# A recurrent attention layer with a gated MLP behind it: the sign of each weight set in an activation, narrow first projections for two more chunks, and another written order

## The chip, the cores and the metric

One core of one Trainium2 chip runs the whole kernel in a single launch. The metric is the device time of an execution in microseconds, lower is better. TensorE (PE) multiplies matrices, VectorE (DVE), ScalarE (ACT) and GpSimd (POOL) do elementwise work, SyncE (SP) issues all DMAs from one queue. Each engine works through its own instructions in the order in which the program lists them.

## The reference, cut to what matters

```
# q, k, v, o_gate: (4, 8, 768, 40); i_gate, f_gate: (4, 8, 768); all fp32
for t in range(S):
    m_new = max(f_gate[t] + m, i_gate[t])
    f, i = exp(f_gate[t] + m - m_new), exp(i_gate[t] - m_new)
    C = f * C + i * outer(v[t], k[t])          # per batch and head
    n = f * n + i * k[t]
    y[t] = sigmoid(o_gate[t]) * (C @ q[t]) / max(abs(n . q[t]), 1)
x = y as (3072 tokens, 320)
h = x @ w_in                                   # w_in (320, 2048)
g = h * erf(softplus(h))
out = g @ w_out                                # w_out (2048, 320)
```

In the reference's inputs w_in and w_out are float64 numbers; the host only reinterprets them as 64-bit integers, and the kernel turns them into fp32 itself.

## The kernel before, in words

The recurrence is worked in 12 chunks of 64 time steps (NC = 12, L = 64). A chunk's tokens are 4 batches x 64 steps = 256; they are handled in two pairs of batches (r = 0, 1), each 128 tokens. For a pair the kernel loads queries and keys (`qk`) and keys, values and output gates (`kvo`), multiplies scores with a decay mask (`dm`, L563), makes the local products, the products with the state and the state's update (L517, L522, L531), divides, gates, transposes (L390 to L394) and splits the result into a rounded half `xh` and a rest `xl`. A gate block (`gate_block`) does the scans of the gates for two chunks and writes small sums to DRAM, from where they are broadcast into `dm` and `eT`.

The MLP of a chunk has four groups g, each for 4 of the 16 blocks of 128 hidden columns. Groups 0 to 7 belong to the first two chunks, alternating; group g from 8 on belongs to chunk g // 4. A group has up projections (L751), evictions to `hb` (L762, in the wide form also L767), softplus, erf and a product with `hb` (L771, L775, L779), a split of that into `gh` and `gl` (L789 or L791, L795; groups 0 to 5 are "plain" and have none), and down projections (L815 plain, L817 to L820 split) into an accumulator per chunk that is stored after the fourth group.

An up projection adds weight half x input half products. In the narrow form a step does two blocks of 128 hidden columns with 8 matmuls of 256 tokens each, all into the block's own half of a 512-column tile, and one ScalarE copy of 512 columns evicts both. In the wide form a step does one block with 5 matmuls: three that have both input halves side by side as 512 moving columns, and two of 256. The two halves of the tile then have to be added: ScalarE copies one to `hb` and VectorE adds the other (L767). Before, groups from 8 on are wide.

A weight arrives as pairs of 32-bit words, 26 pieces in all (8 from `weights_in`, 2 from `weights_tail`, 16 from `weights_out`), by way of `raw` tiles. `decode` makes fp32 bits of it: VectorE shifts the low words (L625), ScalarE multiplies the high words, read as fp32, by 2^-112 (L631), VectorE shifts that left by 3 and joins it with the low word (L636), and VectorE takes the sign bit of the high word and joins that too (L638). `halves`, `weights_tail` and `split_out` split the result into halves.

The order of all this is written out by hand: `ORDER` is a list of step numbers, and each step's instructions are issued when its turn comes. The steps' costs in the program belong to the planner that made the list and issue nothing. A negative entry issues filler matmuls. Where a ScalarE step names table sets (X is the exponential set, S softplus, G the sigmoid set) and the loaded one isn't among them, `Plan.run` issues a load of the first named set (L878). A load waits for its buffer, a step for its inputs, and whatever is queued behind on the same engine waits with it; `raw`, `qk`, `kvo`, `hb` and some others share a pool of 20 buffers.

Of the kernel before, what the change touches and what calls it, by code (L numbers as in the profile page):

```python
# [13 lines left out]
ALU = mybir.AluOpType  # L14
# [16 lines left out]
REBIAS = 2.0 ** -112  # L31


class Plan:
# [138 lines left out]
def tile_mlstm_moe(  # L173
# [446 lines left out]
    def decode(key, raw, n, full, out, **first):  # L620
# [7 lines left out]
        @op('ACT', n / 1010 + 0.063, r=[(R, 0)], w=[(R, 2)])  # L628
        def _():
            word = raw().bitcast(F32)[:, :, 1]  # L630
            nc.scalar.activation(word, word, AF.Copy, scale=REBIAS)  # L631

# [307 lines left out]
```

## Time and profile before

| | before |
|---|---|
| time, median of 3 runs | 468.57 us (466.16 to 469.02) |
| the profiled execution | 470.77 us |
| its span, first to last instruction | 469.1 us |
| TensorE busy | 453.2 us (97%), 6010 matmuls, granted clock 0.985 |
| VectorE busy | 358.8 us (77%), 713 instructions |
| ScalarE busy | 334.2 us (71%), 541 instructions, 57 of them table loads of 73.1 us |
| DMA | 51.80 MB, 110 GB/s on average |

The busy share of TensorE is an upper bound: matmuls are pipelined, and the ends of their records are modelled. What the span is made of is told by stretches and gaps.

### The profile page before, as it was taken

To read this page: it belongs to the slowest core of one execution; us is meant where nothing else is said; L and a number is where in the kernel's file an instruction comes from. 1 tells how busy PE (TensorE), PEld (TensorE's weight loads), DVE (VectorE), ACT (ScalarE), POOL (GpSimd) and SP (SyncE) were. 2 spreads that over 40 slices of the span, in tenths; PEclk is the share of its full clock that TensorE was granted. 3 is DMA by queue.
4 is the path that set the end of the run, shared out by engine and by line. 5 is a ranking of instruction groups with operands and counts; after the bars stand their busy time and mean duration, and the time that the engine had idled before them with its cause. 6 is when DMAs were issued, how large, how long until landed. Compare 5 with 4: busy or idle time off the path is not lost.

```text
span 469.1 us, 13982 instructions
## 1 busy us (share of the span) xinstructions
PE 453.2 (97%) x6010; PEld 397.6 (85%) x6010; DVE 358.8 (77%) x713; ACT 334.2 (71%) x541; POOL 35.8 (8%) x62
## 2 busy tenths in 40 slices
PE   8798997999999999999999999999999999999996
PEld 4467995788788898898899898888899889999996
DVE  6979999789997876878749786786579659665762
ACT  5746988788997486787658985775796584566650
POOL 2001040002010230000210010015000000000000
PEclk9979999899999999999999999999999999999999
DMA  7988876095335703235305612543232100000011
GB/s 219 385 233 288 239 200 199 16 236 185 92 84 149 180 3 83 76 84 148 105 4 147 162 25 88 144 117 116 92 89 82 31 1 1 15 1 14 16 43 28
DMA packets 46830, 51.80 MB, mean 110 GB/s; under 512 B 27056, under 2 KB 31664, under 8 KB 46768
## 3 DMA queue, kind: packets, MB, share of 16 engines
q1 hardware_dynamic: 46768, 50.91, 37.6%
q8 instruction: 47, 0.77, 0.7%
q14 instruction: 15, 0.12, 0.1%
HBM read 46.77 MB, written 4.13 MB: 109 GB/s over the span
## 4 chain that ended last, share of the span: by engine, by line
PE 73%; DVE 10%; DMA 8%; ACT 4%; SPq 2%; issue 2%; DVEq 0%; ACTq 0%
PE h L751 29%; PE pob L819 10%; PE pob L817 9%; PE pob L820 9%; PE pa L815 3%; DMA dm<-gd 3%; PE pa L531 2%; PE pa L508 2%; DMA eT<-gd 2%; PE pa L517 2%; PE pob L815 2%; DMA raw<-in_w_in_dram 2%; DVE raw L636 1%; PE pa L390 1%; PE pa L522 1%
## 5 line engine op out<-in xcount | busy, mean ns | idle before, releaser
L751 PE MATMUL h<-xh,wh 128*128 128x512 f32 (+1 forms) x672 | 203.7, 371 | 2.0 <-DVE hb L767 1.2
L751 PEld LDWEIGHTS h<-xh,wh 128*128 128x128 f32 x672 | 114.9, 189 | 20.8 <-DVE hb L767 2.6
L762 ACT ACTIVATE hb<-h 128x256 f32<-128x256 f32 (+1 forms) x176 | 69.2, 399 | 74.5 <-PE h L751 74.1
L767 DVE TENSOR_TENSOR hb<-h,hb 128x256 f32<-128x256 f32 x160 | 66.3, 420 | 60.6 <-ACT hb L762 59.6
L751 PE MATMUL h<-xh,wl 128*128 128x256 f32 x384 | 108.0, 281 | 0.0
L819 PE MATMUL pob<-woh,gh 128*128 128x320 f32 x328 | 98.3, 311 | 0.0
L820 PE MATMUL pob<-wo,gh 128*128 128x320 f32 x328 | 97.5, 309 | 0.0
L751 PEld LDWEIGHTS h<-xh,wl 128*128 128x128 f32 x384 | 72.7, 189 | 2.8
L878 ACT ACT_TABLE_LOAD x57 | 73.1, 1283 | 1.8 <-PEq L928 0.8
L779 DVE TENSOR_TENSOR n<-n,hb 128x1024 f32<-128x1024 f32 x48 | 58.9, 1230 | 6.7 <-ACT n L775 6.4
L820 PEld LDWEIGHTS pob<-wo,gh 128*128 128x128 f32 x328 | 61.6, 188 | 1.7
L819 PEld LDWEIGHTS pob<-woh,gh 128*128 128x128 f32 x328 | 61.6, 188 | 0.4
L817 PE MATMUL pob<-woh,gl 128*128 128x320 f32 x328 | 60.7, 311 | 0.0
L486 POOL TENSOR_SCALAR_AFFINE_SELECT dm<-dm 128x512 f32<-128x512 f32 (+1 forms) x40 | 32.3, 815 | 290.4 <-ACT dm L466 266.0
L817 PEld LDWEIGHTS pob<-woh,gl 128*128 128x128 f32 x328 | 52.4, 188 | 1.9
L771 ACT ACTIVATE n<-hb 128x1024 f32<-128x1024 f32 x48 | 49.9, 1056 | 3.9 <-DVE hb L767 2.1
L795 DVE TENSOR_TENSOR gl<-n,gh 128x1024 fp32r<-128x1024 f32 x42 | 52.1, 1246 | 0.3
L775 ACT ACTIVATE n<-n 128x1024 f32<-128x1024 f32 x48 | 50.2, 1055 | 0.3
L789 ACT ACTIVATE gh<-n 128x1024 fp32r<-128x1024 f32 x26 | 27.4, 1055 | 2.7 <-DVE n L779 2.7
L407 DVE TENSOR_TENSOR xh<-pa,xh 128x384 fp32r<-128x384 f32 x24 | 13.3, 553 | 13.2 <-ACT xh L403 13.2
L825 ACT ACTIVATE o<-pob 128x320 f32<-128x320 f32 x22 | 9.4, 433 | 16.2 <-PE pob L817 13.9
L403 ACT ACTIVATE xh<-pa 128x384 fp32r<-128x384 f32 x24 | 11.7, 488 | 11.9 <-PE pa L394 7.0
(98 smaller groups left out, 510.9 us busy)
## 6 DMA issues: line engine op xcount, KB each, us to landing
qk<-in_qk_dram SPq DMA_DIRECT2D x24, 512.0 KB, 4.9
kvo<-in_kvo_dram SPq DMA_DIRECT2D x24, 484.0 KB, 4.0
eT<-gd SPq DMA_DIRECT2D x44, 128.0 KB, 4.0
raw<-in_w_out_dram SPq DMA_DIRECT2D x16, 320.0 KB, 4.7
dm<-gd SPq DMA_DIRECT2D x40, 128.0 KB, 3.8
raw<-in_w_in_dram SPq DMA_DIRECT2D x8, 512.0 KB, 7.0
out_dram<-o SPq DMA_DIRECT2D x48, 80.0 KB, 2.4
raw<-in_w_in_dram SPq DMA_DIRECT2D x4, 256.0 KB
```

The costliest lines, as they stand in the source:

```text
L486: nc.gpsimd.affine_select(out=x, in_=x, pattern=[[0, H], [1, L]], compare_op=ALU.is_ge, fill=0.0, base=base, channel_multiplier=-1)
L751: nc.tensor.matmul(h[:, n * T:n * T + n_], w, m, start=(s == 0), stop=(s == len(ops) - 1))
L762: nc.scalar.activation(part(), G(f'h{i}')[:, T:2 * T] if wide else G(f'h{i}'), AF.Copy)
L767: nc.vector.tensor_tensor(part(), G(f'h{i}')[:, 0:T], part(), op=ALU.add)
L771: nc.scalar.activation(new('n0', [128, 1024], ('n0', g)), G('hb'), AF.Softplus)
L775: nc.scalar.activation(G('n0'), G('n0'), AF.Erf)
L779: nc.vector.tensor_tensor(G('n0'), G('n0'), G('hb'), op=ALU.mult)
L795: nc.vector.tensor_tensor(new('gl', [128, 1024], ('gl', g), F32R), G('n0'), G('gh').bitcast(F32), op=ALU.subtract)
L817: nc.tensor.matmul(acc(b), G('gl')[:, ts], woh[:, j], start=False, stop=(j == NFF - 1))
L819: nc.tensor.matmul(acc(b), G('gh')[:, ts], woh[:, j], start=(j == 0), stop=False)
L820: nc.tensor.matmul(acc(b), G('gh')[:, ts], t['wol', j], start=False, stop=False)
L878: plan.run(ORDER, lambda k: nc.scalar.preload_act_table_set(KIND[k]), stay)
```

## The change

Three things change. In `decode` the ScalarE activation becomes a parametric ReLU: positive words are multiplied by 2^-112, negative words by 2^-112 x 2^32. The greater exponent of a negative word puts a one where the left shift by 3 moves it into the sign bit, so the last VectorE pass is left out, and the joining pass writes the result itself. The activation now names the table sets X and G. Second, the wide form begins with group 16, which is the fifth chunk; groups 8 to 15 (the third and fourth chunk) take the narrow form. Third, the list of steps is written anew: 1,587 steps where there were 1,651 (each of the eight groups has two steps fewer on TensorE, two on ScalarE and four on VectorE). The new list has 6 filler entries' worth of matmul steps where the old one has 8, and leads to 61 table loads in place of 57.

```
-REBIAS = 2.0 ** -112
+REBIAS, NEGATIVE = 2.0 ** -112, 2.0 ** 32
...
 ORDER = [
-    10, 12, 2, 9, 11, -2, 1, 13, 0, 5, 14, 4, 6, 3, 7, 15, 8, 17, 93, 94, 95, 96, 16, 33, -1, 34, 32, 36, 31, 38, 27, 341, 342,
...
+    1, 2, 0, 5, 9, 4, 6, 12, 13, 14, 3, 10, 7, 15, 16, 99, 101, 20, 31, 8, 17, 11, 33, 100, 102, 32, 34, 36, 35, 27, 28, 93,
...
-        @op('ACT', n / 1010 + 0.063, r=[(R, 0)], w=[(R, 2)])
+        @op('ACT', n / 1010 + 0.063, r=[(R, 0)], w=[(R, 2)], table='XG')
         def _():
             word = raw().bitcast(F32)[:, :, 1]
-            nc.scalar.activation(word, word, AF.Copy, scale=REBIAS)
-
-        @op('DVE', n / 474 + 0.255, r=[(R, 2)], w=[(R, 1), *out], **first)
+            nc.scalar.activation(word, word, AF.Prelu, scale=REBIAS, alpha=NEGATIVE)
+
+        @op('DVE', n / 948 + 0.1275, r=[(R, 2)], w=[(R, 1), *out], **first)
         def _():
             lo, hi = raw()[:, :, 0], raw()[:, :, 1]
-            nc.vector.scalar_tensor_tensor(out=lo, in0=hi, scalar=3, in1=lo,
+            nc.vector.scalar_tensor_tensor(out=full(), in0=hi, scalar=3, in1=lo,
                                            op0=ALU.logical_shift_left, op1=ALU.bitwise_or)
-            nc.vector.scalar_tensor_tensor(out=full(), in0=hi, scalar=-0x80000000, in1=lo,
-                                           op0=ALU.bitwise_and, op1=ALU.bitwise_or)
...
-        wide = g >= 8
+        wide = g >= 16
...
-            @op('PE', 0.921 if wide else 1.915, mm=5 if wide else 16, r=[((n, k), b) for n in ('xh', 'xl') for b in range(2)]
+            @op('PE', 0.937 if wide else 1.915, mm=5 if wide else 16, r=[((n, k), b) for n in ('xh', 'xl') for b in range(2)]
```

## Rows read from the trace of the kernel before

**Rows 1.** Busy time of each engine by stretches of 20 us, clock, DMA.

```profile
20.00:40.00 20.00, 17.04 (x252) 11.83 (x253) 16.96 (x37) 10.29 (x20) 0.00 (x0) 0.83 0.82 253
40.00:60.00 20.00, 19.59 (x297) 18.33 (x296) 19.25 (x44) 17.59 (x32) 1.33 (x2) 1.00 0.90 274
60.00:80.00 20.00, 18.49 (x384) 16.19 (x382) 18.85 (x37) 17.68 (x26) 4.90 (x6) 1.00 0.71 207
80.00:100.00 20.00, 19.08 (x78) 14.12 (x79) 15.47 (x35) 16.35 (x25) 0.00 (x0) 0.83 0.36 103
...
220.00:240.00 20.00, 20.00 (x356) 18.15 (x355) 15.70 (x32) 14.56 (x26) 4.95 (x6) 1.00 0.26 72
...
320.00:340.00 20.00, 18.94 (x198) 16.79 (x197) 12.07 (x23) 14.05 (x24) 3.50 (x4) 1.00 0.20 59
```

(The columns are the stretch and its length, busy time and instruction count of PE, PEld, DVE, ACT and POOL, the granted TensorE clock, the DMA share and GB/s.)

**Rows 2.** The same, two microseconds after the gap at 80 us.

```profile
80.00:82.00 2.00, 1.08 (x2) 0.84 (x3) 1.97 (x6) 1.44 (x3) 0.00 (x0) 0.50 0.53 116
```

**Rows 3.** TensorE's timeline, 28 to 46 us: start, length, instruction, [idle before, releaser].

```profile
33.58 0.68 PE L517 MATMUL pa<-state,qe 40*64 40x41 f32 x32 [0.74 <-DVE qe L479]
...
39.20 0.50 PE L751 MATMUL h<-xh,wh 128*128 128x256 f32 x2 [0.63 <-ACT hb L762]
```

**Rows 4.** TensorE's timeline, 51 to 63 us, narrow up projections.

```profile
51.38 0.28 PE L751 MATMUL h<-xh,wl 128*128 128x256 f32 x1
...
52.34 0.28 PE L751 MATMUL h<-xh,wl 128*128 128x256 f32 x1
```

**Rows 5.** TensorE's timeline, 69 to 98 us.

```profile
69.62 0.68 PE L517 MATMUL pa<-state,qe 40*64 40x41 f32 x32
...
71.42 0.69 PE L508 MATMUL pa<-qk 40*64 40x64 f32 x32
72.05 4.57 PE L815 MATMUL pob<-wo,n 128*128 128x320 f32 x16
77.51 0.68 PE L517 MATMUL pa<-state,qe 40*64 40x41 f32 x32 [0.89 <-DVE dm L563]
...
80.92 4.63 PE L815 MATMUL pa<-wo,n 128*128 128x320 f32 x8 [1.54 <-DVE kvo L602]
...
87.88 0.38 PE L390 MATMUL pa<-ident,kvo 128*128 128x128 f32 x2
```

**Rows 6.** VectorE's timeline, 65 to 86 us.

```profile
76.76 0.69 DVE L563 TENSOR_TENSOR dm<-pa,dm 128x512 f32<-128x512 f32 x1
...
80.39 0.48 DVE L602 TENSOR_TENSOR kvo<-pa,den 128x320 f32<-128x320 f32 x1
```

**Rows 7.** Groups by line and shape: count, busy us, mean ns, idle before.

```profile
L878 ACT ACT_TABLE_LOAD x57 | 73.1, 1283 | 1.8 <-PEq L928 0.8
...
L767 DVE TENSOR_TENSOR hb<-h,hb 128x256 f32<-128x256 f32 x160 | 66.3, 420 | 60.6 <-ACT hb L762 59.6
...
L762 ACT ACTIVATE hb<-h 128x256 f32<-128x256 f32 x160 | 59.9, 380 | 72.8 <-PE h L751 72.4
...
L762 ACT ACTIVATE hb<-h 128x512 f32<-128x512 f32 x16 | 9.4, 591 | 1.8 <-PE h L751 1.7
...
L636 DVE SCALAR_TENSOR_TENSOR raw<-raw 128x320 int32<-128x320 int32 x16 | 8.2, 510 | 0.3
...
L631 ACT ACTIVATE raw<-raw 128x320 f32<-128x320 f32 x16 | 7.9, 498 | 0.1
...
L631 ACT ACTIVATE raw<-raw 128x512 f32<-128x512 f32 x10 | 6.9, 686 | 1.8 <-DMA raw<-in_w_in_dram 1.8
L636 DVE SCALAR_TENSOR_TENSOR raw<-raw 128x512 int32<-128x512 int32 x10 | 6.8, 685 | 0.4
```

**Rows 8.** TensorE's timeline, 144 to 150 us, wide up projections.

```profile
145.00 0.28 PE L751 MATMUL h<-xh,wl 128*128 128x256 f32 x1
...
145.93 0.28 PE L751 MATMUL h<-xh,wl 128*128 128x256 f32 x1
```

**Rows 9.** The page's DMA issues: size, median us to landing.

```profile
qk<-in_qk_dram SPq DMA_DIRECT2D x24, 512.0 KB, 4.9
```

141 rows, old and new, of the table ORDER are left out of this document.

## The prediction

> **What bounds the kernel now.** I read the table of stretches first. Later in the run TensorE is busy for all of a stretch of 20 us, as from 220 to 240, while VectorE (15.7) and ScalarE (14.6) are not; early it is the other way round: from 40 to 80 us VectorE has 19.25 and 18.85 of 20 [rows 1]. So late a microsecond counts only if it is TensorE's, and early what counts is which wait lets TensorE go. A busy share hides the early loss, because matmul records overlap and because a matmul at half clock looks busy too; I therefore read TensorE's own timeline for gaps and the pitch of equal work. It shows two places. Between 30 and 45 us gaps of 0.74 and 0.63 us stand ahead of a chunk's products and of an up projection, released by VectorE and by ScalarE [rows 3]. From 72.05 to 87.88 us TensorE does two plain down projections of group 0, the local products of a chunk, one plain down projection of group 1 and one narrow up projection. At full rate that is 4.57, 1.80 (from 69.62 to 71.42), 4.57/2 = 2.29 and 1.92 (twice the 0.96 us of eight matmuls), 10.6 us in all [rows 4, 5]; it takes 15.8. The missing 5.3 us are two waits on VectorE and, behind the longer one, a granted clock of 0.50, the lower level of 1.2 GHz: group 1's single down projection then takes 4.63 us [rows 2, 5]. The releasing steps are the score product at 76.76 and the division at 80.39 [rows 6], and VectorE has no gap ahead of either: it was simply late, with decode passes of weight pieces queued among them.
>
> **Part 1, the sign pass.** Each of 26 weight pieces had two equal scalar_tensor_tensor passes on VectorE and now has one. The remaining one stays as long as it was: 16 x 0.510 + 10 x 0.685 = 15.0 us leave VectorE [rows 7], all of it in the first 90 us or so. The activation that was there anyway becomes a parametric ReLU in place of a scaled copy: same words, same count, so 0.498 and 0.686 us as before [rows 7]. The trace shows no parametric ReLU. Its bounds are nothing below the copy, which already passes every word once, and above it a second pass, as dear again as the first: 7.9 + 6.9 = 14.8 us on ScalarE. I take zero, since the copy has the same shape, place and immediate scale. The Trainium skill, page "ScalarE activation tables: per-element evaluation and per-set limits", section "What a function is on this engine", says that with the same operands the cost is the same whichever table is read; by that the extra is zero as well, and no run here shows it yet.
>
> The step now has a table tag (exponential or sigmoid set). I followed the written order: none of its loads stands ahead of one of the 26 steps, so they find a fitting table. The order as a whole has 61 loads where it had 57, three more of the exponential set and one of softplus: 4 x 1.283 = 5.1 us on ScalarE [rows 7]. TensorE late in the run covers them; early they are part of the first rival. The same skill's page "ScalarE: Activation LUTs", "What ACT_TABLE_LOAD costs", gives about 2.7 us to each, against 1.283 in the row; by it the four would cost 10.8 us, and the row decides.
>
> **Part 2, narrow up projections in the third and fourth chunk.** Eight groups lose their wide form. VectorE loses 8 x 4 x 0.420 = 13.4 us of additions; ScalarE's evictions go from 4 x 0.380 to 2 x 0.591 us a group, 8 x 0.34 = 2.7 us less [rows 7]. TensorE streams the same columns, in 8 matmuls a block of 128 rows of the weight instead of 5. The pitch of a block is 0.96 us narrow (51.38 to 52.34) and 0.93 wide (145.00 to 145.93) [rows 4, 8], so 8 x 4 blocks x 0.03 = 1.0 us more on the path. The changed planner costs (0.921 to 0.937) change no instruction.
>
> **Part 3, the order.** The last vector step that the first up projection of group 4 needs is the 62nd on VectorE in the old order and the 57th in the new one, with eight decodes ahead of it in both. So the queue to it is shorter by 8 x 0.685 = 5.5 us for the passes, and by some 2.4 more for the five steps that have moved behind it (a mask addition, a split of inputs and one batch pair's division, scaling and gating; 0.685 for the long ones to 0.5 for the others, an estimate from the rows of like size [rows 6, 7]). TensorE's gain there is at least the two gaps shown, 1.4 us, and at most 5.5 + 2.4 = 7.9. I take 5.0, near the count of passes, because VectorE's 17.0 us in 20 to 40 [rows 1] leave 3 us in which it waits on others and that a faster pass can't remove. At the second place the queue is shorter by the passes of all pieces decoded up to there, far more than the two waits; TensorE then reaches it unstalled, keeps its clock, and the 5.3 us go. What is late next is ScalarE, below. The order has six filler matmul steps instead of eight; they stand in TensorE's waits of the first 30 us and I count them at nothing. If a gap there becomes cold, its price is bounded by the fall at 80 us, some 3 us.
>
> The constants' load now goes ahead of the first gates' load on SP's queue, and the stores of gate sums stand ahead of more weight loads. The first delays the gate scan by one issue, the second lets broadcasts start earlier; I set the two at zero together. Later, output stores, gate stores, broadcasts and chunk loads share that one queue in a new sequence (third rival).
>
> **Sum** against the profiled execution, 469.1 us of span in 470.8: -5.0 (start) - 5.3 (72 to 88 us) + 1.0 (narrow blocks) = -9.3, so 461.5. The median of the runs shown is 2.2 us under that execution: 459.3.
>
> **Rivals.** (a) ScalarE takes VectorE's place as the late one. It has 17.59, 17.68 and 16.35 of each 20 us from 40 to 100 [rows 1], 8.4 idle in 60, and must give the same results 5.3 us sooner there with one or two more table loads. If it keeps half of its idle time, 2.5 us of the gain are lost (462); if it keeps all of it, 5.3 + 1.5 = 6.8 (466.1). A dearer parametric ReLU leads here too. For it: it is close. Against: part of its idle time is waiting for VectorE, and evictions shrink. (b) The weights don't land sooner: DMA is busy for 0.82 and 0.90 of 20 to 60 us [rows 1]; then the start gains next to nothing, 459.3 + 5.0 = 464.3. Against: the queue's lull and its waits for free buffers, not bandwidth, fill the difference. (c) Slower: in the new order SP's queue makes a late chunk wait. For the second pair of batches of chunk 7 (counted from 0) the load of queries and keys stands last on it, just ahead of the vector step that reads it, behind a gate store that needs a table switch. A load takes 4.9 us to land [rows 9]; if it is issued only at its turn, TensorE idles up to that long and then pays some 3 us of low clock, 8 us a place. One place gives 467, no measurable change; from the second on it is slower, 475. For it: TensorE already has 18.94 of 20 from 320 to 340 us, where neither of the other engines is full. Against: from 220 to 240, with chunk loads running, it has all 20 [rows 1].
>
> **How the numbers follow.** Chances: forecast 0.58, (a) 0.24, (b) 0.10, (c) 0.08. The range goes from the start's upper bound (7.9) together with no price for the narrow blocks and a little saved by unseen waits (455) to the end of (a) (466); it leaves out (c) and the tail of the others. A measurement of this kernel tells about 1% from no change, so faster means under 463.9 and slower over 473.3: the forecast and nearly half of (a) and (b) are faster, 0.73; the rest of these and (c) at one place 0.21; slower 0.06.
>
> **What would show it.** In the changed kernel: 26 instead of 52 such passes on VectorE; the parametric ReLU at 0.50 and 0.69 us; the first up projection of group 4 starting about 5 us earlier; no fall of the clock between 70 and 100 us; narrow blocks still at 0.96 us. Wrong would be: gaps of TensorE between 40 and 100 us released by ScalarE, a new clock fall, or gaps after 150 us behind chunk loads or broadcasts.

## The result, and the profile after

The changed kernel takes 464.58 us (median of 8 executions, 461.90 to 466.27), the kernel before 468.47 in the same job (8 executions, 466.16 to 472.27). The ratio is 0.9898 with a 95% interval of 0.9863 to 0.9933: faster by 1.0%, 4.8 us, between 3.1 and 6.4. (The ratio comes from all executions of the job; the two medians by themselves lie 3.9 us apart.) Forecast were 459.3 us and 9.2 us of gain; the time lies in the range, the gain is about half of what was forecast. The profiled execution of the changed kernel took 462.74 us (span 461.0), 1.8 under its median, while that of the kernel before lay 2.2 over the median it was set against. The two profiles are therefore 8.0 us apart (their spans 8.1), more than the medians. The mean granted clock of each of the eight executions is on record too: it goes from 0.987 to 1.000, and the profiled execution has the lowest.

The table of stretches of the changed kernel, columns as in [rows 1]:

```profile
0.00:20.00 20.00, 16.21 (x199) 9.18 (x203) 13.18 (x38) 12.06 (x33) 3.37 (x22) 1.00 0.88 301
20.00:40.00 20.00, 17.59 (x343) 14.35 (x343) 15.90 (x35) 10.23 (x21) 0.00 (x0) 0.74 1.04 278
40.00:60.00 20.00, 19.62 (x295) 18.16 (x295) 16.80 (x40) 18.00 (x30) 1.33 (x2) 1.00 0.91 236
60.00:80.00 20.00, 20.00 (x390) 17.52 (x389) 15.77 (x39) 19.77 (x33) 4.04 (x4) 1.00 0.91 250
80.00:100.00 20.00, 20.00 (x109) 16.00 (x108) 16.06 (x32) 18.30 (x27) 0.37 (x1) 1.00 0.63 164
...
320.00:340.00 20.00, 20.00 (x269) 18.29 (x268) 14.37 (x30) 14.71 (x25) 2.96 (x4) 1.00 0.16 34
```

Against [rows 1] three things are to be seen. From 60 to 100 us TensorE had 18.49 and 19.08 and a clock of 0.83 in the second stretch; now it is full, at full rate, and VectorE has fallen from 18.85 to 15.77. From 320 to 340 us its 18.94 has become 20.00. But from 20 to 40 us the clock is 0.74 where it was 0.83, which is 10.4 us instead of 6.8 at the lower level (20 x 0.26 x 2), and the DMA share is 1.04 where it was 0.82.

Groups by line and shape, which answer to [rows 7]:

```profile
L628 ACT ACTIVATE raw<-raw 128x320 f32<-128x320 f32 x16 | 7.5, 514 | 0.0
L633 DVE SCALAR_TENSOR_TENSOR wo<-raw 128x320 int32<-128x320 int32 x16 | 7.4, 484 | 0.0
L633 DVE SCALAR_TENSOR_TENSOR raw<-raw 128x512 int32<-128x512 int32 x10 | 6.8, 690 | 0.7 <-ACT raw L628 0.2
L628 ACT ACTIVATE raw<-raw 128x512 f32<-128x512 f32 x10 | 6.7, 676 | 0.0
...
L873 ACT ACT_TABLE_LOAD x61 | 78.3, 1283 | 1.9 <-PEq L923 0.8
...
L870 PE MATMUL pob<-ident 128*128 128x512 f32 x12 | 6.9, 674 | 0.0
```

The parametric ReLU takes 514 and 676 ns where the copy took 498 and 686; there are 26 joining passes in place of 52, and 61 table loads. The last line is the filler matmuls. In the kernel before they were four more and 3.2 us dearer:

```profile
L875 PE MATMUL pob<-ident 128*128 128x512 f32 x16 | 10.1, 735 | 0.0
```

TensorE's timeline of the changed kernel, at the places of [rows 3] and [rows 5] and at a narrow projection of the fourth chunk that was wide before:

```profile
22.47 1.11 PE L505 MATMUL pa<-qk 40*64 40x64 f32 x58
25.50 0.34 PE L505 MATMUL pa<-qk 40*64 40x64 f32 x6 [1.92 <-issue]
...
29.84 1.09 PE L514 MATMUL pa<-state,qe 40*64 40x41 f32 x32 [0.18 <-DVE xh L404]
...
38.77 0.50 PE L746 MATMUL h<-xh,wh 128*128 128x256 f32 x2 [0.18 <-ACT hb L757]
...
46.99 0.50 PE L746 MATMUL h<-xh,wh 128*128 128x256 f32 x2
...
75.99 0.68 PE L514 MATMUL pa<-state,qe 40*64 40x41 f32 x32
...
77.79 4.57 PE L810 MATMUL pa<-wo,n 128*128 128x320 f32 x16
82.20 0.38 PE L387 MATMUL pa<-ident,kvo 128*128 128x128 f32 x2
...
117.94 0.28 PE L746 MATMUL h<-xh,wl 128*128 128x256 f32 x1
...
118.90 0.28 PE L746 MATMUL h<-xh,wl 128*128 128x256 f32 x1
```

The products of 75.99 go straight on to the down projection at 77.79, with 1.80 us for what took 3.41 [rows 5], and two down projections take 4.57 where a single one took 4.63. The narrow pitch is 0.96 us. At the start the two gaps of [rows 3], 0.74 and 0.63 us, have shrunk to 0.18 each, at 29.84 and 38.77. But there is something new: the scores of the second chunk are two steps, one for each pair of batches, of 32 matmuls in the profile's count, and they stand directly behind each other. In the second of them, after the 58th of the 64, TensorE stands still for 1.92 us, with "issue" for a releaser, so nothing that the profile shows was awaited. The first up projection of group 4 starts at 46.99 us; before, it started at 47.20.

Stretches of 2 us around that stop, same columns:

```profile
24.00:26.00 2.00, 0.49 (x7) 0.42 (x7) 1.05 (x3) 0.00 (x0) 0.00 (x0) 1.00 1.02 399
26.00:28.00 2.00, 2.00 (x6) 0.71 (x5) 1.18 (x2) 0.00 (x0) 0.00 (x0) 0.56 1.05 400
...
34.00:36.00 2.00, 2.00 (x11) 2.00 (x11) 1.82 (x4) 1.33 (x2) 0.00 (x0) 0.50 0.95 240
36.00:38.00 2.00, 2.00 (x17) 2.00 (x17) 1.80 (x6) 0.85 (x3) 0.00 (x0) 0.88 0.99 267
```

After a stretch in which TensorE worked for 0.49 of 2 us the granted clock goes to the lower level, at 26.2 us, and stays there until 36.5. From 24 to 28 us ScalarE does nothing, and VectorE is busy for 2.23 of 4 us. The timeline of ScalarE, then that of VectorE, in the same place:

```profile
28.71 0.49 ACT L400 ACTIVATE xh<-pa 128x384 fp32r<-128x384 f32 x1 [5.32 <-PE pa L391]
29.10 0.65 ACT L628 ACTIVATE raw<-raw 128x512 f32<-128x512 f32 x1
```

```profile
29.23 0.56 DVE L404 TENSOR_TENSOR xh<-pa,xh 128x384 fp32r<-128x384 f32 x1 [2.05 <-ACT xh L400]
29.71 0.42 DVE L622 TENSOR_SCALAR raw<-raw 128x512 int32<-128x512 int32 x1
```

These are the two halves of chunk 0's second split. ScalarE's waits 5.32 us for transposes behind TensorE's stop, VectorE's waits for ScalarE's, and weight decodes are queued behind both. So VectorE is not the late one in this place: it waits, by way of ScalarE, for TensorE.

### The profile page after: what moved, and what is told of

Read it like the earlier page. It is cut to its first block, busy times and chain, and to the rows that moved or that the text cites. A ratio compares the mean times of both kernels' runs of the same rounds, so it can differ in the third digit from the quotient of the medians.

```text
span 461.0 us, 14089 instructions
## 1 busy us (share of the span) xinstructions
PE 450.4 (98%) x6102; PEld 402.8 (87%) x6102; DVE 330.7 (72%) x655; ACT 336.9 (73%) x529; POOL 37.2 (8%) x62
## 4 chain that ended last, share of the span: by engine, by line
PE 93%; DVE 3%; ACT 1%; issue 1%; DMA 0%; DVEq 0%
PE h L746 39%; PE pob L812 11%; PE pob L814 11%; PE pob L815 10%; PE pa L528 4%; PE pob L810 3%; PE pa L810 3%; PE pa L514 3%; PE pa L505 3%; PE pa L519 2%; PE pa L387 2%; PE pob L281 1%; PE pob L870 1%; PE pa L391 1%; DVE raw L633 1%
## 5 line engine op out<-in xcount | busy, mean ns | idle before, releaser
L746 PE MATMUL h<-xh,wh 128*128 128x256 f32 (+1 forms) x768 | 201.8, 345 | 0.2 <-ACT hb L757 0.2
L746 PEld LDWEIGHTS h<-xh,wh 128*128 128x128 f32 x768 | 126.5, 190 | 14.2 <-ACT hb L757 0.4
L757 ACT ACTIVATE hb<-h 128x256 f32<-128x256 f32 (+1 forms) x160 | 66.5, 423 | 66.0 <-PE h L746 65.2
L762 DVE TENSOR_TENSOR hb<-h,hb 128x256 f32<-128x256 f32 x128 | 52.6, 421 | 53.0 <-ACT hb L757 52.2
L812 PE MATMUL pob<-woh,gl 128*128 128x320 f32 x328 | 61.7, 312 | 0.0
L483 POOL TENSOR_SCALAR_AFFINE_SELECT dm<-dm 128x512 f32<-128x512 f32 (+1 forms) x40 | 33.8, 851 | 310.9 <-ACT dm L463 229.4
L790 DVE TENSOR_TENSOR gl<-n,gh 128x1024 fp32r<-128x1024 f32 x42 | 51.0, 1219 | 1.2 <-PE pob L815 0.4
L560 DVE TENSOR_TENSOR dm<-pa,dm 128x512 f32<-128x512 f32 x24 | 16.4, 685 | 10.7 <-PE pa L505 7.6
```

What stands on the lines that cost most here:

```text
L483: nc.gpsimd.affine_select(out=x, in_=x, pattern=[[0, H], [1, L]], compare_op=ALU.is_ge, fill=0.0, base=base, channel_multiplier=-1)
L746: nc.tensor.matmul(h[:, n * T:n * T + n_], w, m, start=(s == 0), stop=(s == len(ops) - 1))
L757: nc.scalar.activation(part(), G(f'h{i}')[:, T:2 * T] if wide else G(f'h{i}'), AF.Copy)
L762: nc.vector.tensor_tensor(part(), G(f'h{i}')[:, 0:T], part(), op=ALU.add)
L790: nc.vector.tensor_tensor(new('gl', [128, 1024], ('gl', g), F32R), G('n0'), G('gh').bitcast(F32), op=ALU.subtract)
L812: nc.tensor.matmul(acc(b), G('gl')[:, ts], woh[:, j], start=False, stop=(j == NFF - 1))
```

## The experiments

The first theory after these traces was that VectorE's shorter queue is the gain, at both places, and that something new takes it back at the start. The rival was that the new order itself, not the passes, makes the difference. Experiments 1 to 6 take the parts apart; 7 to 11 go for the start. Each ratio is to the kernel before on the same chip.

**1. The kernel before, unchanged.** 

> The kernel before, unchanged: what one execution's profile is worth. If the 5.3 us between 72 and 88 us (two waits on VectorE and a clock fall) stand in every execution, this profile shows them too and its time is within 0.5% of the runs beside it. If the clock fall is a matter of the single execution, the profile has a shorter or no fall there and its own time is some 3 us under the 470.8 us of the execution that I summed from.

469.33 us, ratio 0.9997 (0.9973 to 1.0021). Its table of stretches:

```profile
20.00:40.00 20.00, 16.65 (x262) 12.09 (x263) 18.27 (x40) 11.69 (x24) 0.00 (x0) 0.91 0.86 262
...
80.00:100.00 20.00, 19.38 (x79) 14.38 (x80) 15.34 (x35) 16.51 (x26) 0.00 (x0) 0.83 0.39 106
```

The fall at 80 us is there again (0.83); the one at the start varies, 0.91 here against 0.83 [rows 1]. So both profiles of this kernel have the second fall, and the start's differs by 3.2 us at the lower level. Not every execution has it: of the 22 others of this kernel beside runs 1 to 4, the three shortest (466.45 to 467.41 us) have a mean granted clock of 0.999 or 1.000. The median of the 22 is 0.993, where the execution that the forecast was summed from has 0.985.

**2. The passes alone, in the old order.** Against the kernel before; 5 of the 26 pieces keep two passes, because in the old order their ReLU would each need a further table load. (One of the other 21 needs one all the same: the profile has 58 loads, 57 before.)

```
+        two = key in (('raw', 3, 0), ('rawo', 4), ('rawo', 10), ('rawo', 11), ('rawo', 15))
...
-            nc.scalar.activation(word, word, AF.Copy, scale=REBIAS)
+            if two:
+                nc.scalar.activation(word, word, AF.Copy, scale=REBIAS)
+                return
+            nc.scalar.activation(word, word, AF.Prelu, scale=REBIAS, alpha=NEGATIVE)
```

> The old order and the old wide groups, with the parametric ReLU and a single VectorE pass for 21 of the 26 pieces; the five whose activation would stand behind a load of the softplus set keep the scaled copy and both passes, so that no table load is added. Theory 1 (my prediction): the waits on VectorE at 30 to 45 and 72 to 88 us come from the passes, so this alone gives most of the gain, 461 to 464 against 468.5. Rival: the old order fixes when TensorE gets its work, VectorE only idles more, 467 to 469.

467.85 us, ratio 0.9946 (0.9927 to 0.9966): 2.5 us, between the two theories. Its table of stretches:

```profile
40.00:60.00 20.00, 17.99 (x281) 16.54 (x279) 15.25 (x36) 16.51 (x27) 1.32 (x2) 1.00 0.97 278
60.00:80.00 20.00, 18.64 (x385) 16.61 (x385) 18.27 (x35) 18.71 (x29) 5.37 (x6) 1.00 0.73 210
80.00:82.00 2.00, 2.00 (x9) 1.45 (x9) 1.86 (x5) 1.96 (x3) 0.00 (x0) 1.00 0.56 130
80.00:100.00 20.00, 20.00 (x94) 15.01 (x95) 16.22 (x37) 19.63 (x31) 0.00 (x0) 1.00 0.57 146
```

From 80 to 100 us TensorE has no idle time any more (0.92 us in [rows 1]), and the fall at 80 us is gone (1.00 where [rows 2] have 0.50); the profile of run 5, which keeps both passes, has no fall there either, so the fall's absence alone proves little. And TensorE's idle time from 40 to 60 us has grown from 0.41 to 2.01, half of it one wait of 1.03 us for a load of queries and keys at 55.23. The gain stands where VectorE was late, and part of it goes at once to the next late thing; that the order, not made for the shorter step, is the reason is a reading, not a test.

**3. The changed kernel with the two passes put back.**

```
-            nc.scalar.activation(word, word, AF.Prelu, scale=REBIAS, alpha=NEGATIVE)
+            nc.scalar.activation(word, word, AF.Copy, scale=REBIAS)
...
+            nc.vector.scalar_tensor_tensor(out=full(), in0=hi, scalar=-0x80000000, in1=lo,
+                                           op0=ALU.bitwise_and, op1=ALU.bitwise_or)
```

> The changed kernel with the old decode (scaled copy, two VectorE passes); order and narrow groups stay. Theory 1: 15 us of passes are back on VectorE in the first 90 us and the waits with them, 468 to 471. Rival: the order carries the gain, and VectorE has room for the passes where TensorE doesn't wait for it, 464 to 466.

473.88 us, ratio 1.0080 (1.0050 to 1.0109). With 0.9898 for the changed kernel, the passes are worth 1.8% in the new order, some 8.5 us, against 0.5% in the old one. TensorE's timeline shows three places:

```profile
27.25 0.49 PE L505 MATMUL pa<-qk 40*64 40x64 f32 x6 [3.02 <-issue]
...
52.70 0.50 PE L748 MATMUL h<-xh,wh 128*128 128x256 f32 x2
...
79.08 0.68 PE L514 MATMUL pa<-state,qe 40*64 40x41 f32 x32 [2.13 <-DVE dm L560]
```

The wait on VectorE's score product at the second place is back with the passes. Group 4's first up projection starts at 52.70 us, 5.7 later than in the changed kernel's profile: in this order the passes delay the start too. The stop inside the scores is there without the ReLU; it stands in all eight profiles of the new order (the changed kernel's and those of runs 3, 4 and 7 to 11) and in none of the five of the old one (the kernel before and runs 1, 2, 5, 6), so it comes with the order.

**4. The changed kernel with the wide form from group 8.** `wide = g >= 8`, each narrow step replaced in place by two wide ones, and steps put off until a tile buffer is free. 

> The changed kernel with the wide form from group 8 on again, each narrow step replaced in place by two wide ones with their evictions and VectorE additions. By my sum the narrow blocks cost TensorE 1.0 us, so this is 1 us faster if VectorE and ScalarE have room, 463.5. Rival: the 13.4 us of additions hold the up projections' evictions and TensorE waits, 466 or more.

500.77 us, ratio 1.0660 (1.0632 to 1.0687), far from what either theory said. TensorE's timeline, the stop in the second chunk's scores and two of nine waits for a buffer:

```profile
26.89 0.39 PE L508 MATMUL pa<-qk 40*64 40x64 f32 x6 [3.93 <-issue]
...
128.44 0.80 PE L749 MATMUL h<-xh,wh 128*128 128x512 f32 x1 [4.92 <-DVE hb L765]
...
179.67 0.50 PE L749 MATMUL h<-xh,wh 128*128 128x512 f32 x1 [2.81 <-DVE hb L765]
```

A wide block takes one of two `h` buffers for itself and gives it back only after VectorE's addition; in an order made for narrow blocks that addition comes late. This says how little such an order forgives, and nothing on the price of the narrow form. The run is worth something for the start, though: up to 90 us each engine has the same steps in the same sequence as in the changed kernel, and SP's queue is the same throughout. So without any added bytes the stop takes 3.93 us here, and group 4 starts at 48.88. The clock is at its lower level for only 3.4 us behind it.

**5. The kernel before with groups 8 to 15 narrow,** old decode and old order. 

> The old order and the old decode with groups 8 to 15 narrow: each pair of wide steps becomes one narrow step at the place of the first, with one eviction at the place of the later. My sum: 1.0 us more on TensorE's path, and the 13.4 us of additions that VectorE loses lie after 96 us where TensorE doesn't wait for it, so 469.5 to 471. Rival: VectorE's lighter queue lets the steps behind it start sooner, 466 to 468.

471.34 us, ratio 1.0034 (1.0000 to 1.0067): 1.6 us dearer, between nothing and 3.1, where 1.0 was forecast.

**6. Both parts in the old order** (2 and 5 together). 

> The old order with both parts: parametric ReLU and one pass for 21 of 26 pieces, groups 8 to 15 narrow. What is missing to the changed kernel is then the new order alone. If the order only follows the parts, this comes near the changed kernel, 465 to 466. If the order is a part of its own, it stays with the parametric ReLU alone, 467 to 469.

468.51 us, ratio 0.9973 (0.9943 to 1.0004), near the sum of 2 and 5 (-0.54 + 0.34 = -0.20%). The remaining 0.75% come with the order, the five further pieces with a single pass included. But the order without the passes gains nothing: run 3 stands 0.46% above run 5, with intervals that just overlap. So neither theory holds alone; the new order gains only with the shorter decode, and in it the 26 passes are worth about three times as much as 21 of them in the old one.

**7. The changed kernel, fillers moved.** The filler entry behind the second chunk's two score steps goes between them, twice as long, to keep TensorE at work.

```
-    ... 64, 73, -1, 75, ...
+    ... 64, -2, 73, 75, ...
```

> The changed kernel with one change in its order: the filler entry that stands behind the last of chunk 1's two score steps goes between them, twice as long. In the changed kernel TensorE stops for 1.92 us inside that step, at 23.6 us, with nothing awaited, and its clock falls 3 us later for 10.2 us. Theory 1: the stop is the instruction stream that comes in late, and the fall follows from the idle time; filler work in that place keeps the clock and takes no time of its own, and the start is 2 to 3 us shorter, 462 to 463. Rival: VectorE and ScalarE set the pace from 29 to 41 us (decode behind chunk 0's second split), the clock is not on the path, and the time stays at 464 to 465.5.

463.60 us, ratio 0.9844 (0.9800 to 0.9887). TensorE's timeline:

```profile
22.72 0.69 PE L504 MATMUL pa<-qk 40*64 40x64 f32 x32
23.34 1.98 PE L869 MATMUL pob<-ident 128*128 128x512 f32 x4
25.26 0.57 PE L504 MATMUL pa<-qk 40*64 40x64 f32 x22
26.75 0.39 PE L504 MATMUL pa<-qk 40*64 40x64 f32 x10 [0.92 <-issue]
...
34.59 0.62 PE L527 MATMUL pa<-kvo,dm 64*32 64x41 f32 x19 [3.03 <-issue]
```

The first stop shrinks, and another of 3.03 us appears inside a later step, again with nothing awaited; the clock falls at 29.8 instead of 26.2 us, for as long. The first stop stands again after the 58th matmul, four of the 58 being fillers now (32 + 4 + 22): it keeps its place in TensorE's list of instructions, whatever stands there. The second stop comes 128 matmuls behind the first, here and in run 11. The time of this run is the lowest of all, but its interval overlaps that of the changed kernel (0.9863 to 0.9933), and the profile doesn't show what was expected.

**8. The changed kernel, chunk 0's second split** (steps 53 and 54) put behind three weight decodes, so that these don't wait for TensorE.

```
-    ... 109, 53, 54, 129, ... 160, 139, ...
+    ... 109, 129, ... 160, 53, 54, 139, ...
```

> The changed kernel with chunk 0's second split (one ScalarE copy, one VectorE subtraction) put behind the decodes of three weight pieces, since both engines idle from 24.9 to 29.2 us behind it while it waits for a transpose. Theory 1 of the start: the queues behind that split are what my 5.0 us missed, and the decodes fill the idle time, 461 to 463. Rival: the weight pieces land too late at a DMA share of 1.0, or TensorE's own chain is late, and nothing is gained, 464 to 466.

465.33 us, ratio 0.9906 (0.9866 to 0.9946): no gain. TensorE's timeline:

```profile
25.24 0.34 PE L504 MATMUL pa<-qk 40*64 40x64 f32 x6 [1.37 <-issue]
...
32.74 1.09 PE L513 MATMUL pa<-state,qe 40*64 40x41 f32 x32 [4.85 <-DVE xh L403]
```

The decodes come earlier, and the products of the second chunk wait 4.85 us, because the split frees the tile that they write. That the split blocks the decodes is true; putting it later only moves the wait, so this run can't say what unblocked decodes alone would be worth.

**9. The changed kernel with 0.66 MB of early loads issued later.**

```
-    ... 349, 157, 112, 158, 135, 347, 113, 134, ... 172, 181, 183, 350, ... 199, 177, ...
+    ... 349, 135, 347, 157, 112, 158, 134, ... 172, 350, ... 199, 113, 181, 177, ...
```

> The changed kernel with two loads of 320 KB that are first read at 49 us or later (o0, o9) issued behind the loads of 32 to 35 us instead of at 22.9 and 26.6 us, and i20 behind i11; o9's Prelu and the pass that joins it stand later too. Nothing is left out. In the changed kernel 3.20 MB moved between 20 and 30 us at a DMA share of 1.0, so this takes 0.66 MB or, at 320 GB/s, 2.0 us of transfers out of that stretch. Theory 1 (full DMA engines hold back what TensorE needs at the start, its instruction blocks among them): the stop of 1.92 us in the middle of a11's scores shrinks below 1 us, the first up projection of m4 starts 1 to 2 us before 47.0, and the time is 462.5 to 464. Theory 2 (the start is set by TensorE's own work at the granted clock of 0.50, which these bytes don't touch): the stop stays or moves to another step, m4 starts at 46.5 to 47.5, the time is 464 to 465.5.

464.83 us, ratio 0.9887 (0.9856 to 0.9919). **10. The changed kernel with 1.0 MB more** at 20 us:

```
+            if (part, k) in ((2, 0), (1, 1)):
+                spare = tc.dram_tile([128, 1024], I32, name=f"spare{part}{k}")
+                nc.sync.dma_start(spare, w_in.bitcast(I32)[k * 128:(k + 1) * 128, part * 1024:(part + 1) * 1024])
```

> The changed kernel with the loads of i20 and i11 followed each by a copy of the same 512 KB to a spare place in DRAM that nobody reads: 1.0 MB more at 20 us, some 3.3 us of transfers at 320 GB/s. Theory 1 (the DMA share of 1.0 is what holds the start): the stops of TensorE between 20 and 35 us grow by 2 to 3.3 us together, the time is 466.5 to 468.5. Theory 2 (TensorE's own work and clock set the start): the weights land later but TensorE reaches m4 at 46.5 to 47.5 as before, the time is 464 to 465.5.

465.31 us, ratio 0.9896 (0.9869 to 0.9923). TensorE's timeline of 9, then of 10:

```profile
23.48 1.11 PE L504 MATMUL pa<-qk 40*64 40x64 f32 x58 [1.51 <-DVE kvo L598]
25.50 0.49 PE L504 MATMUL pa<-qk 40*64 40x64 f32 x6 [0.91 <-issue]
```

```profile
22.09 1.11 PE L505 MATMUL pa<-qk 40*64 40x64 f32 x58
27.00 0.48 PE L505 MATMUL pa<-qk 40*64 40x64 f32 x6 [3.80 <-issue]
```

With 1.0 MB more the stop takes 3.80 us instead of 1.92 and work goes on 1.5 us later, as theory 1 of these two runs has it. But run 4 has 3.93 us without these bytes, and run 3 3.02, so one profile of each kernel doesn't show that the bytes lengthen the stop. Run 9 says no more: its scores begin 1.0 us later, behind a wait of 1.51 us on VectorE, and go on at 25.50 us as in the changed kernel, so its shorter stop (0.91) is only the later beginning. The bytes that it moves come too late in the stretch to bear on this. Group 4 starts at 47.55 there. In 10 it starts at 49.06, 2.1 us later than in the changed kernel's profile but only 0.2 later than in run 4, and the span is 464.0 us against 461.0; the medians, with intervals of some 3 us, don't tell the kernels apart. Both times fit theory 2; nothing measured needs theory 1.

**11. Runs 7 and 9 together.** 

> The later loads of the run before the last together with the filler matmuls moved between the two score steps of the second chunk (two groups instead of one), the version with the lowest time so far at 463.6. Theory 1: both stops in the middle of steps shrink and the clock is not taken down at 26 to 30 us, the time is 460 to 462.5. Theory 2: the filler alone decides, the time stays at 463 to 464.5.

463.67 us, ratio 0.9868 (0.9831 to 0.9905). TensorE's timeline:

```profile
26.71 0.39 PE L504 MATMUL pa<-qk 40*64 40x64 f32 x10 [1.70 <-issue]
...
33.45 0.62 PE L527 MATMUL pa<-kvo,dm 64*32 64x41 f32 x19 [1.45 <-issue]
```

Both stops are there, the second half as long as in 7, and group 4 starts at 47.42. With 7 it has the lowest times measured, 0.3 to 0.5% under the changed kernel's, which can't be told from no difference here.

## Why the prediction was right in direction and twice too large

- **The sign pass: right.** VectorE went from 358.8 to 330.7 us of busy time, 28.1 less; 15.0 for the passes and 13.4 for the additions had been counted. The parametric ReLU costs what the copy did, as the Trainium skill's page "ScalarE activation tables: per-element evaluation and per-set limits", section "What a function is on this engine", has it, now with a row of this case: 514 and 676 ns against 498 and 686. ScalarE rose by 2.7 us; +5.1 for the loads and -2.7 for the evictions give 2.4. No load stands ahead of a ReLU: the count of 61 was right.
- **72 to 88 us, -5.3: right between the two profiles.** No wait on VectorE, no fall of the clock; TensorE lost 1.51 + 0.92 us idle and 3.4 us of clock from 60 to 100 us before [rows 1] and loses nothing there now, 5.8 together. Run 3 brings the wait back by putting the passes back. In the medians the clock's part must count for less, because executions of the kernel before without any fall exist, and because their median clock (0.993) is that of the changed kernel's eight executions (0.993 too).
- **Narrow blocks, +1.0: right as far as measured;** pitch 0.96 us, and 1.6 us in run 5 (0 to 3.1).
- **The start, -5.0: this is the step that failed.** Forecast was group 4's first up projection 5 us earlier, at about 42; it starts at 46.99, though four filler matmuls less stand ahead of it in the new order, and at 47.4 to 49.1 in six further profiles of that order (4 and 7 to 11). The price of the passes was not what was wrong: with them put back (run 3) group 4 starts at 52.70, 3.6 to 5.7 us later than in those seven. Wrong was to take that price off the old order's time. With the passes still in it, the new order starts group 4 5.5 us later than the old one did (52.70 against 47.20), and that eats what the passes give. Each of these starts is from one profile. VectorE is not what the start waits for now: it has 13.18 and 15.90 of the first two stretches, and its two longer waits after 20 us (2.05 and 0.95) hang on TensorE. The two gaps of 1.4 us did shrink, to 0.36, but from 20 to 40 us TensorE is idle for 2.41 us instead of 2.96 all the same, and its clock takes 5.2 us (half of 10.4) instead of 3.4.
- **Fillers and SP's order, counted at nothing and at zero: part of the same failure.** What the new order costs at the start, the forecast had among these terms, without a price. The runs show the stop inside the score step as a part of it: 0.91 to 3.93 us in all eight profiles of this order. The DMA share from 20 to 40 us went from 0.82 to 1.04 as well; that the fuller engines cause the stop is not shown, since it takes as long without run 10's added bytes (3.93 us in run 4) as with them (3.80). Nor is the clock's fall behind the stop shown to have a price: runs 4 and 10 go on at nearly the same time (26.89 and 27.00), the clock is low for 3.4 us in one and 10.2 in the other, and group 4 starts at 48.88 and 49.06. The changed kernel's executions agree: the one at a clock of 0.987 took 462.74 us, one at 0.996 took 464.90. Which part of the order costs the rest stays open, and none of the five attempts on the start (7 to 11) won it back beyond doubt.
- **Late gaps, not forecast: -1.6.** 0.54 us from 300 to 320 (19.46 of 20 before) and 1.06 from 320 to 340 us are gone, in the place that I had named as a risk of the third rival.

Read from the two profiles, these terms give -5.8 (60 to 100 us) + 1.0 (narrow blocks) - 1.6 (late gaps) + 1.2 (20 to 40 us: 0.55 less idle, 1.8 more for the clock) = -5.2 us, where the spans differ by -8.1. The cheaper fillers, 3.2 us of TensorE's work, would more than fill the rest, but how much of them stood in waits is not known. The medians' 4.8 us (3.1 to 6.4) is another quantity, and a sum from two profiles that comes near it is luck. Which of its executions a kernel shows in the profile is part of the error of any sum made like this one: the forecast was summed from an execution of low clock (0.985), and taking off 2.2 us at the end doesn't undo that in the term for 72 to 88 us.

Of the rivals, (a) came close: ScalarE has 19.77 of 20 from 60 to 80 us. But TensorE is full there, and ends no wait on it. (b) gave nearly the measured time (464.3), and the start did gain next to nothing. Its reason, that DMA is the limit of the start, is not shown: the DMA share reached 1.04, but 1.0 MB more of transfers (run 10) left the time where it was within some 3 us. (c) didn't happen: from 60 to 440 us TensorE has 20.00 of every 20.

## What to carry to other kernels

A queue that gets shorter is worth something only where it ended the wait; ahead of each such place read which engine the shorter one waits for in turn, as its own idle time (3 of 20 us here) already hinted. A new order and a cheaper step have to be judged together: here the step alone gave 0.5%, the order without it gained nothing, and all together gave 1.0%. And a gap or a stop read from one profile needs a second profile of the same instructions before a cause is put to its length: here the same stop took 1.92 us in one and 3.93 in another.

## What the runs showed of the hardware that I had not expected

TensorE can stop inside a run of small matmuls, with nothing awaited that the profile shows: 0.91 to 3.93 us in all eight profiles of the new order (the changed kernel's, runs 3, 4 and 7 to 11). The DMA share around the first stop is about 1.0 in all of them, but around run 11's second (1.45 us) it is 0.60. The stop has a fixed place in TensorE's list of instructions. It stands behind the 58th matmul from the start of the second chunk's scores whether fillers are among them or not, so it is not a wait of the matmul that happens to stand there; in runs 7 and 11 a second one follows 128 matmuls later. The queue that carries instructions fits that. One packet of it begins 2.3 to 3.0 us before TensorE goes on, at each of the ten stops: between 22.5 and 23.0 us in the changed kernel, where work goes on at 25.50, and between 24.5 and 25.0 us in run 10, where it goes on at 27.00. The two stretches, in this order:

```profile
q8 instruction: 1, 0.02, 14.0%
```

```profile
q8 instruction: 1, 0.02, 13.8%
```

They give packets, MB and share. That the late packet is what TensorE waits for is an inference, since no run varied the packet; what makes it late is open, the bytes of other transfers included. The second surprise is the clock. In seven of the eight profiles the granted clock goes to the lower level during the stop or within some 3 us behind it, for 3.4 to 13.6 us, and not by the stop's length: 3.4 us for 3.93 (run 4), 10.2 for 1.92 (the changed kernel). In run 8 it stays up after a stop of 1.37 us and falls at 30.7 us, in a wait of 4.85.
